# Reordering the prologue of an attention-and-MLP kernel: query transpositions ahead of the last value sums, with more dummy matmuls between

## The chip, the cores and the metric

The kernel runs on one core of one Trainium2 chip. The metric is the device time of one execution in microseconds (us), as the median of several runs. A profile of one execution shows, for each engine, when every instruction ran: TensorE (PE, and PEld for its weight loads), VectorE (DVE), ScalarE (ACT), GpSimd (POOL) and SyncE (SP).

## The reference

Eight batches of eight heads, 576 queries each, head size 64. Keys and values are averaged over groups of eight rows first, so that 72 pooled rows remain. Attention over them gives the input of an MLP with a SiLU:

```python
def _attn_ref(q, k, v):
    pool = 8
    k_p = k.reshape(B, H, Sp, pool, D).mean(axis=3)
    v_p = v.reshape(B, H, Sp, pool, D).mean(axis=3)
    scores = scale * np.matmul(q, k_p.transpose(0, 1, 3, 2))
    attn = softmax(scores)            # over the 72 pooled keys
    return np.matmul(attn, v_p)       # (8, 8, 576, 64)

x = attn_out.transpose(0, 2, 1, 3).reshape(4608, 512)
h = x @ w_in                          # 512 -> 2048
out = (h * sigmoid(h)) @ w_out        # 2048 -> 512
```

## The kernel before

The MLP walks over 4608 tokens in nine tiles of 512 (loop `for t in range(NT)`); each tile has an up stage (`up`, w_in and SiLU) and a down stage (`down` in the first tile, `down_quarters` after it). A batch is 576 tokens, so the attention of the next batch is run inside the MLP of the current tile: its steps are `fillers` with due times, which `spread` puts between the MLP matmuls. Nothing else is scheduled: `tc.manual_schedule()` leaves the instructions of every engine in the order in which the code issues them, and semaphores alone hold an engine back.

The attention of batch 0 has no MLP to hide in. It is the prologue (lines 705 to 770), and its order is written out by hand. The 576 queries are treated as two halves `f` of 288 columns, the eight heads as two groups `g` (or `a`) of four. `part(g, f)` is one quarter of the work. For each quarter:

- `q_transpose(b, a, f)` (L153, DVE) puts queries into `qT`.
- `scores(b, segs)` (L351, PE) multiplies `qT` with pooled keys `kz` into four PSUM tiles `sc_ps`, one per head, and ACT takes four exponentials into `es` (L359).
- `denominators` (L369, PE) sums `es` over the pooled keys. Reciprocals are taken on ACT as exp(-ln) (L378, L379), or on DVE (L375) for the second query half.
- `numerators` (L395, PE) multiplies `es` with pooled values `vp`, and DVE multiplies by the reciprocals into `xT` (L404), the input of the MLP. The first MLP tile begins with columns 0 to 287, the first query half; the second half's denominators and numerators are fillers of its up stage.

Keys and values are pooled by DVE additions in `slot_sums(name, j)` (L274, L278): rows lie in five slots of 128, slots 0 to 2 are `j=0`, the others `j=1`. `select_k(b, a)` (L296) and `select_v(b, a)` (L314) are small matmuls that pick the rows of four heads into PSUM, and `copy_k` (L303) and `copy_v` (L321) bring them to `kz` and `vp`; each call says whether ACT (`act_copy`) or DVE copies.

`warm_up(n)` issues n dummy matmuls of 128x512 on zeros into a PSUM tile that nobody reads (L703). The prologue holds 37 of them.

PSUM has three buffers under the tag `mm` (dummies, hidden tiles `hp_ps`, some numerators) and five under `at` (scores, denominators, other numerators). A tile takes the next buffer of its tag in turn, and waits until that buffer's last reader is done. In the prologue the `at` tiles are, in order of issue, one `kz_ps`, four scores, four scores, two denominators, and so on, so the scores of one quarter follow the readers of earlier ones.

Transfers of the prologue are issued ahead of all this by SP, ACT and POOL (queries by POOL, in four pieces; values by POOL in three). On ACT the exponentials and the SiLU belong to different table sets; `moe_tables()` loads the second one (L414) ahead of the first up stage.

Of the kernel before, what the change touches and what calls it, by code (L numbers as in the profile page):

```python
# [36 lines left out]
def kernel(  # L37
# [53 lines left out]
    def ps_tile(shape, dtype, tag, name):  # L91
        return psum.tile(shape, dtype, tag=tag, bufs=banks[tag], name=name)
# [57 lines left out]
    def q_transpose(b, a, f):  # L150
        st = batches[b]
        n = QF * D
        nc.vector.transpose(  # L153
            out=st["qT"][:, a, f * QF : (f + 1) * QF].rearrange("r i c p -> r (i c p)"),
            in_=st["q_bf"][:, a, f * n : (f + 1) * n],
        )
# [94 lines left out]
    def load_slots(eng, b, name, i0, i1, half=None):  # L251
        es = slice(0, RE) if half is None else slice(half * RE // 2, (half + 1) * RE // 2)
        src = (k if name == "k" else v)[b].rearrange("h (sp p) d -> (h sp) (p d)", p=POOL)
        src = src[:, es]
        how = dict(accum_op=ALU.add) if half else {}
        tiles = row_tiles[name]
        w = es.stop - es.start
        if i0 == SLOTS:
            eng.dma_start(
                out=tiles[1][:REST, SLOTS - SA, :w], in_=src[128 * SLOTS :], **how  # L260
            )
        else:
            j = i0 // SA
            eng.dma_start(
                out=tiles[j][:, i0 - SA * j : i1 - SA * j, :w],
                in_=src[128 * i0 : 128 * i1].rearrange("(i r) e -> r i e", r=128), **how
            )

    def slot_sums(name, j, halves=False):
        raw = row_tiles[name][j]  # L270
        dst = rows5[name][:, SA:] if j else rows5[name][:, :SA]
        w = RE // 4 if halves else RE // 2
        while w > D:
            nc.vector.tensor_add(  # L274
                out=raw[..., :w], in0=raw[..., :w], in1=raw[..., w : 2 * w]
            )
            w //= 2
        nc.vector.tensor_add(out=dst, in0=raw[..., :D], in1=raw[..., D : 2 * D])  # L278


    def segments(h):
        r = SP * h
        while r < SP * (h + 1):
            i = r // 128
            e = min(SP * (h + 1), 128 * (i + 1))
            yield i, (128 if i < SLOTS else REST), r - 128 * i, r - SP * h, e - r
            r = e

    def select_k(b, a):
        st = batches[b]  # L290
        if a == 0:
            st["kz_ps"] = ps_tile([128, 2, 2, SP], FP32, "at", "kz_ps")
        for c in range(2):
            for s in range(4):
                for i, n, r, sp, m in segments(4 * a + s):
                    nc.tensor.matmul(  # L296
                        st["kz_ps"][32 * s : 32 * (s + 1), a, c, sp : sp + m],
                        lhsT=k5[:n, i, c * DH : (c + 1) * DH],
                        rhs=ident[:n, r : r + m], start=True, stop=True,
                    )  # L300

    def copy_k(b, a, copy=nc.vector.tensor_copy):
        copy(out=kz[b % 2][:, a], in_=batches[b]["kz_ps"][:, a])  # L303

    def select_v(b, a, tag="at"):
        st = batches[b]
        if a == 0:
            st["v_ps"] = ps_tile([128, H, D], FP32, tag, "v_ps")
            st["vp"] = mid.tile([SP, H, D], BF16, tag="vp", name="vp")
        for h in range(4 * a, 4 * (a + 1)):  # L310
            segs = list(segments(h))
            for j, (i, n, r, sp, m) in enumerate(segs):
                x = SP + r - sp
                nc.tensor.matmul(  # L314
                    st["v_ps"][:SP, h, :], lhsT=shifts[:n, x : x + SP], rhs=v5[:n, i],
                    start=(j == 0), stop=(j == len(segs) - 1),
                )

    def copy_v(b, a, copy=nc.vector.tensor_copy):
        hs = slice(4 * a, 4 * (a + 1))  # L320
        copy(out=batches[b]["vp"][:, hs, :], in_=batches[b]["v_ps"][:SP, hs, :])  # L321
# [3 lines left out]
    def part(g, f):  # L325
        return ((g, f * QF, (f + 1) * QF),)
# [6 lines left out]
    def width(segs):  # L333
        return QP * sum(i1 - i0 for _, i0, i1 in segs)

    def seg_cols(segs):
        o = 0
        for g, i0, i1 in segs:
            n = QP * (i1 - i0)
            yield g, i0, i1, slice(o, o + n)  # L340
            o += n

    def scores(b, segs):
        st = batches[b]
        w = width(segs)
        sc = [ps_tile([128, 512], FP32, "at", "sc_ps")[:SP, :w] for s in range(4)]
        for g, i0, i1, cs in seg_cols(segs):
            for c in range(2):
                for s in range(4):
                    rows = slice(32 * s, 32 * (s + 1))  # L350
                    nc.tensor.matmul(  # L351
                        sc[s][:, cs],
                        lhsT=kz[b % 2][rows, g, c, :],
                        rhs=st["qT"][rows, g, i0:i1, c, :],
                        start=(c == 0), stop=(c == 1),
                    )
        es = mid.tile([SP, 4, VW], BF16, tag="es", bufs=4, name="es")[:, :, :w]
        for s in range(4):
            nc.scalar.activation(es[:, s, :], sc[s], func=AF.Exp, scale=score_scale)  # L359
        st["es", segs] = es  # L360


    def denominators(b, segs, on_dve=False):
        st = batches[b]
        w = width(segs)
        es = st["es", segs]
        den_ps = ps_tile([128, 512], FP32, "at", "den_ps")
        for s in range(4):
            nc.tensor.matmul(  # L369
                den_ps[32 * s : 32 * (s + 1), :w],  # L370
                lhsT=ones, rhs=es[:, s, :], start=True, stop=True,
            )
        rec = mid.tile([128, VW], FP32, tag="rec", bufs=4, name="rec")[:, :w]
        if on_dve:
            nc.vector.reciprocal(rec, den_ps[:, :w])  # L375
        else:
            lnd = mid.tile([128, VW], FP32, tag="lnd", name="lnd")[:, :w]
            nc.scalar.activation(lnd, den_ps[:, :w], func=AF.Ln)  # L378
            nc.scalar.activation(rec, lnd, func=AF.Exp, scale=-1.0)  # L379
        st["rec", segs] = rec  # L380

    def numerators(b, segs, tags=("at", "at")):
        st = batches[b]
        w = width(segs)
        g0, i0, i1 = segs[0]
        c0 = b * S % NX + i0 * QP
        cols = slice(c0, c0 + (i1 - i0) * QP)
        es = st.pop(("es", segs))
        rec = st.pop(("rec", segs))
        nu = []  # L390
        for c in range(2):
            nu_ps = ps_tile([128, 512], FP32, tags[c], "nu_ps")
            for g, _, _, cs in seg_cols(segs):
                for s in range(4):
                    nc.tensor.matmul(  # L395
                        nu_ps[32 * s : 32 * (s + 1), cs],
                        lhsT=st["vp"][:, 4 * g + s, c::2],
                        rhs=es[:, s, cs],
                        start=True, stop=True,
                    )  # L400
            nu.append(nu_ps)
        ng = len(segs)
        for c in range(2):
            nc.vector.tensor_mul(  # L404
                out=xT[:, 2 * g0 + c : 2 * (g0 + ng - 1) + c + 1 : 2, cols],
                in0=nu[c][:, :w].rearrange("r (g n) -> r g n", g=ng),
                in1=rec.rearrange("r (g n) -> r g n", g=ng),
            )
# [292 lines left out]
    def warm_up(n):  # L701
        for _ in range(n):
            nc.tensor.matmul(warm_ps, lhsT=warm[:, :128], rhs=warm, start=True, stop=True)  # L703
# [33 lines left out]
    act_copy = nc.scalar.copy  # L737
# [3 lines left out]
    copy_k(0, 0, act_copy)  # L741
    warm_up(4)
    q_transpose(0, 0, 0)
    scores(0, part(0, 0))
    slot_sums("k", 1)
    warm_up(3)
    select_k(0, 1)
    copy_k(0, 1, act_copy)
    q_transpose(0, 1, 0)
    warm_up(2)  # L750
    scores(0, part(1, 0))
    denominators(0, part(0, 0))
    slot_sums("v", 0)
    warm_up(2)
    select_v(0, 0, "mm")
    copy_v(0, 0, act_copy)
    denominators(0, part(1, 0))
    q_transpose(0, 0, 1)
    scores(0, part(0, 1))
    slot_sums("v", 1)  # L760
    warm_up(1)
    numerators(0, part(0, 0), ("mm", "at"))
    warm_up(2)
    select_v(0, 1, "mm")
    copy_v(0, 1)
    q_transpose(0, 1, 1)
    warm_up(2)
    numerators(0, part(1, 0), ("mm", "at"))
    scores(0, part(1, 1))
    warm_up(2)  # L770
    load_slots(nc.gpsimd, 1, "k", 0, 3)
    load_slots(nc.gpsimd, 1, "k", 3, 4)
    load_slots(nc.gpsimd, 1, "k", 4, 5)
# [147 lines left out]
```

## Time and profile before

| | |
|---|---|
| median of 3 runs | 289.03 us (288.86 to 289.22) |
| profiled execution | 288.86 us, its span 287.0 us |
| PE busy | 279.4 us, 97% of the span |
| DVE busy | 225.6 us, 79% |
| ACT busy | 183.4 us, 64% |
| POOL busy | 52.6 us, 18% |
| first MLP matmul (L546) starts | 18.12 us after the span's start |
| fourth hidden tile of the up stage starts | 20.85 us |
| PE's granted clock | full in all 40 slices |

The span is the time from the first to the last instruction of the program on the core; the execution's own time also holds what lies around it. Busy time of PE is modelled from the starts of pipelined matmuls, so two neighbouring matmuls can overlap in it; starts are more reliable than ends. A chain of waits is the sequence of work that ended last, followed back from the last instruction, at each step to what released it. In the records a few matmuls can be missing: 35 dummy matmuls are recorded, with 37 weight loads for them.

### The profile page before, as it was taken

The numbers are of one execution on the slowest core, as the hardware profiler recorded it, in microseconds if no ns is written. First come the engines' busy times: TensorE is split into PE (matmuls) and PEld (weight loads), VectorE is DVE, ScalarE is ACT, GpSimd is POOL, SyncE is SP. The second block draws the span as 40 slices with busy tenths as digits, with TensorE's granted clock in tenths as the row PEclk, the third lists the DMA queues.
The fourth block names the chain that finished last, engine by engine and source line by source line (L and its number), as shares of the span: only waits on it lengthen the run. The fifth ranks groups of instructions, "written<-read, shape, count | busy, mean of one in ns | idle before, by whom it ended". The sixth has DMA issues, their size and how long they took to land.

```text
span 287.0 us, 6919 instructions
## 1 busy us (share of the span) xinstructions
PE 279.4 (97%) x2773; PEld 196.0 (68%) x2793; DVE 225.6 (79%) x403; ACT 183.4 (64%) x359; POOL 52.6 (18%) x68
## 2 busy tenths in 40 slices
PE   8989999999999999999999999999999999999995
PEld 2438544466777677767888886687667867786684
DVE  3987854979969896979797969886988786846773
ACT  1577676468656876688568857794679558325700
POOL 8754317501020011101020107212000000000000
PEclk9999999999999999999999999999999999999999
DMA  8999999893749566973979396968830032006004
GB/s 210 269 262 231 217 310 172 221 216 53 148 67 208 124 91 106 136 209 60 140 122 211 73 151 112 164 121 162 161 77 0 2 86 63 2 5 142 2 1 148
DMA packets 35296, 37.70 MB, mean 131 GB/s; under 512 B 9952, under 2 KB 27616, under 8 KB 35264
## 3 DMA queue, kind: packets, MB, share of 16 engines
q0 software_dynamic: 21760, 20.86, 43.1%
q1 hardware_dynamic: 12928, 15.48, 22.3%
q10 hardware_dynamic: 576, 0.92, 1.1%
q8 instruction: 22, 0.36, 0.6%
q14 instruction: 10, 0.08, 0.1%
HBM read 36.70 MB, written 9.44 MB: 161 GB/s over the span
## 4 chain that ended last, share of the span: by engine, by line
PE 91%; DVE 4%; ACT 2%; issue 1%; DVEq 0%
PE hp_ps L546 23%; PE o_psP L654 15%; PE o_psQ L654 15%; PE u_psQ L488 7%; PE u_psP L488 6%; PE o_psR L654 5%; PE sc_ps L351 4%; PE warm_ps L703 4%; PE o_ps L581 3%; PE nu_ps L395 3%; PE den_ps L369 2%; PE u_psR L488 2%; DVE rr_sb L508 1%; ACT r_sb L505 1%; DVE w_sum L632 1%
## 5 line engine op out<-in xcount | busy, mean ns | idle before, releaser
L546 PE MATMUL hp_ps<-xT,w_in_sb 128*128 128x512 bf16 (+3 forms) x397 | 80.8, 338 | 1.4 <-ACT h_T L552 0.4
L552 ACT ACTIVATE h_T<-hp_ps 128x512 bf16<-128x512 f32 (+2 forms) x95 | 51.3, 545 | 27.2 <-PE hp_ps L546 26.3
L654 PEld LDWEIGHTS <-h_sum 128*128 128x128 bf16 x640 | 60.6, 98 | 11.9 <-issue 1.3
L546 PEld LDWEIGHTS <-w_in_sb 128*128 128x128 bf16 x412 | 39.3, 98 | 24.9 <-issue 1.4
L614 DVE TENSOR_TENSOR h_sum<-h_T 128x1024 bf16<-128x1024 bf16 (+1 forms) x72 | 50.8, 743 | 7.0 <-ACT h_T L552 7.0
L359 ACT ACTIVATE es<-sc_ps 72x384 bf16<-72x384 f32 (+1 forms) x100 | 39.0, 470 | 10.0 <-PE sc_ps L351 10.0
L488 PEld LDWEIGHTS <-w_sum 128*128 128x128 bf16 x300 | 29.3, 98 | 8.2 <-DVE x_sum L455 0.5
L654 PEld LDWEIGHTS <-h_T 128*128 128x128 bf16 x256 | 24.1, 98 | 4.4 <-issue 0.9
L496 ACT ACTIVATE h_T<-c_sb 128x512 bf16<-128x512 f32 x30 | 18.8, 628 | 11.6 <-DVE c_sb L520 11.6
L404 DVE TENSOR_TENSOR xT<-nu_ps,rec 128x384 bf16<-128x384 f32 (+1 forms) x50 | 24.0, 533 | 0.4
L378 ACT ACTIVATE lnd<-den_ps 128x384 f32<-128x384 f32 (+1 forms) x23 | 11.1, 484 | 20.2 <-PE den_ps L369 20.2
L153 DVE STREAM_TRANSPOSE qT<-q_bf 128x576 bf16<-128x576 bf16 x32 | 23.0, 754 | 0.0
L182 POOL DMA_DIRECT2D raw<-in_k_dram x5 | 7.0, 1405 | 66.3 <-DVE qT L153 31.2
L274 DVE TENSOR_TENSOR raw<-raw 128x384 f32<-128x384 f32 (+3 forms) x20 | 12.3, 616 | 7.2 <-DMA raw<-in_v_dram 3.6
L654 PE MATMUL o_psP<-w_out_sb,h_sum 128*128 128x256 bf16 x128 | 17.6, 273 | 0.0
L654 PE MATMUL o_psQ<-w_sum,h_sum 128*128 128x256 bf16 x128 | 16.7, 273 | 0.0
L654 PE MATMUL o_psQ<-w_out_sb,h_sum 128*128 128x256 bf16 x128 | 16.6, 273 | 0.0
L654 PE MATMUL o_psP<-w_sum,h_T 128*128 128x256 bf16 x128 | 16.5, 273 | 0.0
L654 PE MATMUL o_psQ<-w_sum,h_T 128*128 128x256 bf16 x128 | 16.5, 273 | 0.0
L182 POOL DMA_DIRECT2D raw<-in_v_dram x5 | 6.9, 1390 | 49.4 <-DMA raw<-in_v_dram 15.6
L654 PE MATMUL o_psR<-w_sum,h_sum 128*128 128x256 bf16 x128 | 15.7, 273 | 0.0
L558 POOL DMA_DIRECT2D out_dram<-o_sb x1 | 0.6, 628 | 81.8 <-issue 81.8
(77 smaller groups left out, 435.9 us busy)
## 6 DMA issues: line engine op xcount, KB each, us to landing
out_dram<-o_sb SPq DMA_DIRECT2D x128, 64.0 KB, 3.0
q_bf<-in_q_dram POOLq DMA_DIRECT2D x6, 576.0 KB, 11.1
raw<-in_k_dram SPq DMA_DIRECT2D x6, 512.0 KB, 5.7
raw<-in_k_dram POOLq DMA_DIRECT2D x5, 576.0 KB, 9.6
raw<-in_v_dram POOLq DMA_DIRECT2D x5, 576.0 KB, 9.1
raw<-in_v_dram SPq DMA_DIRECT2D x5, 512.0 KB, 8.2
w_in_sb<-in_moe_w_in_dram POOLq DMA_DIRECT2D x8, 256.0 KB, 8.3
w_out_sb<-in_moe_w_out_dram POOLq DMA_DIRECT2D x4, 512.0 KB, 13.8
```

The source lines that it names most:

```text
L153: nc.vector.transpose(out=st["qT"][:, a, f * QF : (f + 1) * QF].rearrange("r i c p -> r (i c p)"), in_=st["q_bf"][:, a, f * n : (f + 1) * n],)
L182: nc.gpsimd.dma_start(out=batches[b][f"{name}_raw"], in_=source(b, name)[:, :, PH:], accum_op=ALU.add,)
L274: nc.vector.tensor_add(out=raw[..., :w], in0=raw[..., :w], in1=raw[..., w : 2 * w])
L351: nc.tensor.matmul(sc[s][:, cs], lhsT=kz[b % 2][rows, g, c, :], rhs=st["qT"][rows, g, i0:i1, c, :], start=(c == 0), stop=(c == 1),)
L359: nc.scalar.activation(es[:, s, :], sc[s], func=AF.Exp, scale=score_scale)
L404: nc.vector.tensor_mul(out=xT[:, 2 * g0 + c : 2 * (g0 + ng - 1) + c + 1 : 2, cols], in0=nu[c][:, :w].rearrange("r (g n) -> r g n", g=ng), ...
L488: nc.tensor.matmul(ps[bank][:, u, :], lhsT=w[:, kk, 128 * u : 128 * (u + 1)], rhs=x[:, kk, :], start=first and u == 0 and kk == 0, stop=kk ...
L496: nc.scalar.activation(h_T[:, g : g + 2, j * NQ : (j + 1) * NQ], src, func=AF.Silu)
L546: nc.tensor.matmul(hp_ps[:, r0:r1], lhsT=w_in_sb[:, kk, g * 128 : (g + 1) * 128], rhs=xT[:, kk, x0 : x0 + r1 - r0], start=(kk == 0), stop= ...
L552: nc.scalar.activation(h_T[:, g, n0 : n0 + n], hp_ps[:, :n], func=AF.Silu)
L614: nc.vector.tensor_tensor(out=h_sum[n][:, ks, :], in0=quarter(*a, ks), in1=quarter(*b, ks), op=op)
L654: nc.tensor.matmul(ps[b][:, c, :], lhsT=left(n, kt, c), rhs=W_OUT[n][:, kt, :], start=b not in begun, stop=kt == k1 - 1, skip_group_check= ...
```

## The change

Four things in the prologue change; the rest of the kernel is the same text, and its instructions stand in the same order.

- `scores` takes a callable `between`, which it calls ahead of its fourth exponential. The first scores use it for the sums, selection and ACT copy of the second half of the keys. PE's and DVE's orders stay as they were there; on ACT that copy moves ahead of the fourth exponential.
- The first value copy goes from ACT to DVE and stands behind the transposition `q_transpose(0, 1, 1)`, ahead of `slot_sums("v", 1)`.
- On DVE both transpositions of the second query half stand ahead of that copy and of `slot_sums("v", 1)`. Before, the second of them stood behind these sums, two products and the second value copy.
- On PE the last scores, `part(1, 1)`, move ahead of `select_v(0, 1)` and the numerators of `part(1, 0)`; before, they were behind both. Dummy matmuls are spread otherwise: 45 in place of 37.

```diff
-    def scores(b, segs):
+    def scores(b, segs, between=None):
...
         for s in range(4):
+            if s == 3 and between:
+                between()
             nc.scalar.activation(es[:, s, :], sc[s], func=AF.Exp, scale=score_scale)
...
     q_transpose(0, 0, 0)
-    scores(0, part(0, 0))
-    slot_sums("k", 1)
-    warm_up(3)
-    select_k(0, 1)
-    copy_k(0, 1, act_copy)
+
+    def rest_k():
+        slot_sums("k", 1)
+        warm_up(3)
+        select_k(0, 1)
+        copy_k(0, 1, act_copy)
+
+    scores(0, part(0, 0), rest_k)
     q_transpose(0, 1, 0)
     warm_up(2)
     scores(0, part(1, 0))
     denominators(0, part(0, 0))
     slot_sums("v", 0)
-    warm_up(2)
+    warm_up(3)
     select_v(0, 0, "mm")
-    copy_v(0, 0, act_copy)
+    q_transpose(0, 0, 1)
     denominators(0, part(1, 0))
-    q_transpose(0, 0, 1)
+    warm_up(1)
     scores(0, part(0, 1))
+    warm_up(3)
+    q_transpose(0, 1, 1)
+    copy_v(0, 0)
     slot_sums("v", 1)
+    numerators(0, part(0, 0), ("mm", "at"))
     warm_up(1)
-    numerators(0, part(0, 0), ("mm", "at"))
-    warm_up(2)
+    scores(0, part(1, 1))
+    warm_up(4)
     select_v(0, 1, "mm")
     copy_v(0, 1)
-    q_transpose(0, 1, 1)
     warm_up(2)
     numerators(0, part(1, 0), ("mm", "at"))
-    scores(0, part(1, 1))
-    warm_up(2)
+    warm_up(3)
```

## The prediction, made before the result was known

> **What bounds the kernel now.** The page first: engine shares, then the slices.
>
> ```profile
> PE 279.4 (97%) x2773; PEld 196.0 (68%) x2793; DVE 225.6 (79%) x403; ACT 183.4 (64%) x359; POOL 52.6 (18%) x68
> ...
> PE   8989999999999999999999999999999999999995
> ...
> PEclk9999999999999999999999999999999999999999
> ```
>
> TensorE is busy 97% of the span, at full granted clock in every slice; the only thin slices are the first few and the last. The change sits in the prologue, up to about 20 us, so the question is whether the stream that follows can absorb a shift. The table by stages (columns: window, its length, busy us of PE, PEld, DVE, ACT, POOL, clock, DMA share, GB/s) answers that, together with the list of what PE waited for from 21 us to the end, of which the second longest entry is shown after it (engine, line, releaser: us in total, times, longest):
>
> ```profile
> 12.10:18.10 6.00, 5.51 (x64) 2.42 (x62) 4.95 (x11) 4.56 (x15) 3.97 (x6) 1.00 1.22 200
> 18.10:20.85 2.75, 2.35 (x22) 1.22 (x20) 2.03 (x2) 2.72 (x7) 1.48 (x2) 1.00 1.17 296
> 20.85:35.20 14.35, 14.30 (x135) 9.81 (x136) 11.43 (x23) 10.13 (x25) 5.75 (x9) 1.00 1.19 229
> ```
>
> ```profile
> PE u_psR L488 <- ACT r_sb L505: 0.2, 1, 0.2
> ```
>
> From 20.85 us PE is full (14.30 of 14.35), and after that its waits are a few tenths, on engines that themselves follow PE; none is a wait for a transfer. So the time at which PE gets past the last prologue wait, 20.85 us, moves the end one for one. I then read the chain of waits through that stretch (start, length, what):
>
> ```profile
> 13.54 0.28 PE den_ps L369
> 13.82 0.41 PE sc_ps L351 x8
> 14.24 0.32 PE warm_ps L703
> ...
> 14.57 0.61 PE nu_ps L395 x8
> 15.19 0.54 PE warm_ps L703 x2
> 15.72 0.33 PE v_ps L314 x6
> ...
> 16.15 0.42 DVE vp L321
> 16.57 0.70 DVE qT L153
> ...
> 17.31 0.48 PE sc_ps L351 x8
> 17.79 1.29 ACT es L359 x4
> ...
> 19.09 1.28 ACT L414
> ...
> 20.39 0.42 ACT h_T L552
> ...
> 20.85 0.41 PE hp_ps L546 x2
> ```
>
> The chain leaves PE at 16.15: the copy of the second value half, the last query transposition, the last scores, their four exponentials, the table load, the first SiLU. Then PE, out of PSUM for a fourth hidden tile, goes on at 20.85.
>
> **Paces.** Start to start in the timeline of PE: a dummy 0.22 us (two from 17.68 to 18.12); eight scores 0.37 (17.31 to 17.68), 0.08 more when dummies stand ahead (four dummies 8.53 to 9.49, 0.96); eight numerators 0.36; six value selections 0.33 (chain). From the first MLP matmul (18.12) to the point where the fourth hidden tile could begin PE needs 2.16 (the third tile's last matmul starts at 20.16, its successor could 0.12 later; the stretch includes both fillers of denominators). On ACT: an exponential 0.29 apart and 0.41 long; ln, then its exponential 0.45 later, the next instruction 0.35 after that. On DVE: transposition 0.77 long, 0.70 apart.
>
> **What PE waits for now, from 13.54 (last denominator matmul) to 20.85, 7.31 us.** Work: rest of that matmul 0.21, scores 0.37, seven dummies 1.54, two numerator groups 0.72, value selection 0.33, scores 0.37, MLP 2.16: 5.70. So 1.61 is waiting: 0.18 for the first value copy on ACT (14.39 to 14.57), 0.19 for a PSUM bank held by a logarithm, 0.21 for the second value copy, 0.33 for the transposition, 0.57 for the SiLU, 0.13 in uneven issue.
>
> **The change, part by part.**
> *Third exponential and K copy.* The copy of the second K half is put ahead of the fourth exponential of the first scores. It now starts 11.29, when its matmuls (ending 11.26) release it, and that exponential ended 11.26: the copy cannot start sooner. The exponential moves to about 11.5 to 11.9; the denominators that read it start 12.10, so it costs nothing; without that 0.2 us of cover it would delay them one for one. Gain nothing.
> *Value copy from ACT to DVE.* ACT loses 0.25 (14.17 to 14.42), so the second ln starts 14.17, and the next exponentials 14.96 instead of 15.21, the last ending 16.26. DVE does two transpositions from 12.23 (the query half is needed by 12.93, and DVE's transfer wait of 0.46 at 13.0 is filled by it), then the copy to about 14.1, then the last value sums, 1.48 long, to 15.6 instead of 14.93. Queued behind them are the first products, needed by nobody before the first MLP matmul. All DVE extras are covered: PE wants the copy at 15.08 and the sums at 17.5.
> *Dummies.* 37 become 45. One of the eight falls into the wait for exponentials that ends at 13.54; seven, 1.54 us, come after it.
> *PE's new order.* From PE free at 13.75: dummy and scores(0,1) to 14.42, three dummies to 15.08, numerators to 15.44, a dummy, scores(1,1) at 15.74. These need the PSUM banks of the exponentials above: the fourth bank is free at 16.26, PE issues at 16.30, and goes on at 16.65 (second half, 0.14 plus 0.21) where 16.11 was possible: a new wait of 0.54. It is bounded below by 0 (ACT ahead), above by 0.79 (without the 0.25 that ACT saves); I take 0.54, since every ACT term is a row. Then four dummies to 17.53 and the value selection to 17.86. As now, 0.10 passes before the copy and 0.05 after its 0.42, so numerators start at 18.47, where two dummies end at 18.30: wait 0.17 (between 0 and 0.21, today's). Numerators to 18.83, three dummies, first MLP matmul at 19.49, 1.37 later than now. The products that it reads end 1.34 after the numerators begin, 19.81; the third MLP matmul, the first to read the second head group, comes behind a denominator group at 20.07. No wait.
> *ACT's end.* Last exponentials 16.76 to 18.06, table load to 19.36: 1.0 earlier than now. The first hidden tile is summed only at 20.74, so SiLU waits for PE, and the fourth hidden tile starts unhindered at 19.49 + 2.16 = 21.65.
> *Sum.* 21.65 - 20.85 = +0.80. By the ledger: seven dummies 1.54, two switches 0.16, waits 0.71 instead of 1.61: again +0.80. What is late next: reciprocals on DVE start 1.3 later; the K sums of the next batch then end at about 28.6, the selections that read them come at 28.57 and 29.65 plus 0.80, the first needing only the first sums (27.3). Covered by 0.8 to 2 us. POOL's transfers keep their order and wait for transfers up to 33 us.
>
> **Two rules weighed.** The granted clock reads 1.00 in all stages, and dummies have the same 0.22 us after a 0.33 us wait as before it. The Trainium skill, "TensorE: Matmul & The Clock Gate", Part 1 (HAM oscillation), says that the clock falls only after PE idles for a window of about 3.4 us; it speaks against this change, as the longest wait here is 0.57, so by it a dummy buys nothing; were clock at stake, each such window at half speed would cost 1.7. The table load shows as 1.28, starting 0.02 after the exponentials. "ScalarE: Activation LUTs" (What ACT_TABLE_LOAD costs) adds a drain, 2.66 in all; by that the load would end at 20.72, still ahead of 20.74, and the sum would not move.
>
> **Rivals.**
> *Dummies are free (faster).* If the seven after 13.54 run beside the groups that follow, PE is 1.54 earlier, the MLP begins at about 17.95, and the fourth hidden tile at 20.11: -0.74. For: PE's waits show 1.61 us that could hold them. Against: they stand in order, seven of them behind the new waits, at 0.22 each. It turns faster as soon as the first MLP matmul starts before 18.69. 288.3 us.
> *The new PSUM wait is absent (no change).* 0.80 - 0.54 = +0.26, 289.3. For: it hangs on one ScalarE sequence. Against: its banks' order is fixed by the program.
> *Both ends lose (much slower).* The 0.57 wait is not saved but comes back as a wait for late vector results (reciprocals, K sums): +1.37, 290.4. For: DVE has no gap from 20 to 28.6. Against: the covers above.
> That the change doesn't do what it says isn't open: the built order shows both transpositions ahead of the sums and 45 dummies.
>
> **How the numbers follow.** The profiled execution took 288.86 us around its span of 287.0, 0.17 below the median of 289.03; 288.86 + 0.80 = 289.66 for it, 289.83 as median. 0.2%, about what a measurement of this kernel can tell from no change, is 0.58. Forecast 0.70, its own range 289.4 to 290.3 (waits at their bounds, uneven issue of 0.1 to 0.2 per group); free dummies 0.08; absent wait 0.12; both ends lose 0.10. The forecast's lower end falls within 0.58 for about 0.10 of its 0.70. Faster 0.08, same 0.22, slower 0.70. Range 289.0 to 290.6.
>
> **What would show it.** After: scores(1,1) held by ACT near 16.3; table load over near 19.4; first MLP matmul near 19.5; no SiLU wait at its fourth tile; that tile near 21.65; 45 dummy weight loads; clock 1.00. Wrong if the first MLP matmul comes before 18.7, or PE shows new waits after 22 us.

## The result, and the profile after

| | before | changed |
|---|---|---|
| median (6 runs each) | 288.91 us (287.84 to 289.22) | 290.44 us (289.72 to 290.75) |
| ratio | | 1.0057 (1.0035 to 1.0079) |
| profiled execution, its span | 288.86 us, 287.0 us | 290.32 us, 288.2 us |

The changed kernel is slower, by about 1.5 us where 0.80 was forecast. The median lies in the range given, 289.0 to 290.6, but above the narrower 289.4 to 290.3 that the prediction gave its own sum. What the sum forecast and the rest of the difference can be read apart.

First the profile of the changed kernel: page, then the stages (same columns as before, cut at its own marks), then what PE waited for from 21 us on.

```profile
PE 280.0 (97%) x2781; PEld 196.2 (68%) x2801; DVE 225.9 (78%) x404; ACT 183.4 (64%) x358; POOL 52.4 (18%) x68
...
PE   7999999999999999999999999999899999999995
...
PEclk9999999999999999999999999999999999999999
```

```profile
18.66:20.82 2.16, 2.16 (x22) 1.22 (x21) 1.70 (x2) 0.71 (x2) 1.47 (x2) 1.00 1.15 347
20.82:35.20 14.38, 14.33 (x138) 9.81 (x137) 12.02 (x25) 10.11 (x25) 5.61 (x9) 1.00 1.19 226
```

```profile
PE u_psR L490 <- DVE x_sum L457: 1.1, 2, 0.7
```

The first MLP tiles now run without any gap (2.16 busy of 2.16), but a wait for the input sums `x_sum`, 1.1 us in two places, is new, and the twenty-ninth slice shows it: an 8, at 202 to 209 us.

Then the prologue, PE's timeline of the changed kernel (start, length, engine, line, what, count, idle before):

```profile
7.42 0.28 PE L296 MATMUL kz_ps<-shifts,k 128*32 128x72 bf16 x12 [0.50 <-DVE k L278]
...
15.05 0.80 PE L351 MATMUL sc_ps<-qT,kz 32*72 32x288 bf16 x8
16.00 0.81 PE L705 MATMUL warm_ps<-warm 128*128 128x512 bf16 x3 [0.16 <-issue]
16.65 0.48 PE L314 MATMUL v_ps<-v,shifts 128*72 128x64 bf16 x6
17.06 0.61 PE L705 MATMUL warm_ps<-warm 128*128 128x512 bf16 x2
17.64 0.43 PE L397 MATMUL nu_ps<-es,vp 72*32 72x288 bf16 x8
18.00 0.82 PE L705 MATMUL warm_ps<-warm 128*128 128x512 bf16 x3
18.66 0.41 PE L548 MATMUL hp_ps<-xT,w_in_sb 128*128 128x288 bf16 x2
```

and ACT's, same columns:

```profile
14.11 1.28 ACT L361 ACTIVATE es<-sc_ps 72x288 bf16<-72x288 f32 x4
15.79 1.30 ACT L361 ACTIVATE es<-sc_ps 72x288 bf16<-72x288 f32 x4 [0.40 <-PE sc_ps L351]
17.11 1.28 ACT L416 ACT_TABLE_LOAD   x1
19.69 0.41 ACT L554 ACTIVATE h_T<-hp_ps 128x288 bf16<-128x288 f32 x1 [1.30 <-PE hp_ps L548]
```

The absolute times can't be set beside those of before: here the first key selection starts at 7.42 us, there at 8.32, because the 19 dummies ahead of it reach their full pace sooner. Counted from it, the fourth hidden tile starts 12.53 us later before (20.85) and 13.40 later now (20.82). So the prologue costs 0.87 more, and in this profile the earlier head hid it: at 20.8 us the two kernels are level. The 1.27 us by which the profiled spans differ arise after that, most of them at the two waits for input sums.

### The profile page after: what moved, and what is told of

Read it like the earlier page. It is cut to its first block, busy times and chain, and to the rows that moved or that the text cites. A ratio compares the mean times of both kernels' runs of the same rounds, so it can differ in the third digit from the quotient of the medians.

```text
span 288.2 us, 6934 instructions
## 1 busy us (share of the span) xinstructions
PE 280.0 (97%) x2781; PEld 196.2 (68%) x2801; DVE 225.9 (78%) x404; ACT 183.4 (64%) x358; POOL 52.4 (18%) x68
## 5 line engine op out<-in xcount | busy, mean ns | idle before, releaser
L548 PEld LDWEIGHTS <-w_in_sb 128*128 128x128 bf16 x412 | 39.3, 98 | 24.4 <-issue 0.8
L182 POOL DMA_DIRECT2D raw<-in_k_dram x5 | 7.0, 1404 | 68.6 <-DMA raw<-in_k_dram 29.7
L490 PEld LDWEIGHTS <-w_in_sb 128*128 128x128 bf16 x120 | 11.7, 97 | 6.0 <-issue 2.0
L182 POOL DMA_DIRECT2D raw<-in_v_dram x5 | 6.9, 1389 | 47.5 <-DVE raw L188 23.3
```

The source lines that it names most:

```text
L182: nc.gpsimd.dma_start(out=batches[b][f"{name}_raw"], in_=source(b, name)[:, :, PH:], accum_op=ALU.add,)
L490: nc.tensor.matmul(ps[bank][:, u, :], lhsT=w[:, kk, 128 * u : 128 * (u + 1)], rhs=x[:, kk, :], start=first and u == 0 and kk == 0, stop=kk ...
L548: nc.tensor.matmul(hp_ps[:, r0:r1], lhsT=w_in_sb[:, kk, g * 128 : (g + 1) * 128], rhs=xT[:, kk, x0 : x0 + r1 - r0], start=(kk == 0), stop= ...
```

## The experiments

Times are medians; a ratio is to the kernel before, on the same chip, with its 95% interval. The experiments' runs were made in three groups on three chips, on which the kernel before took 288.67, 289.03 and 289.33 us, so two times from different groups are compared more safely by their ratios. Two lengths are taken from each trace: *prologue*, from the first key selection to the start of the fourth hidden tile, and *rest*, from there to the start of the last matmul. Theory P: the prologue costs the forecast's 0.8 and the rest of the difference is late waits for keys. Theory C: the change itself lengthens the later work. Theory S: the prologue costs all of it.

**Both kernels again.** No edit.

> The changed kernel once more. Theory P (the prologue costs +0.8 us, the rest of the measured +1.5 is lost later, where VectorE waits for the keys of a later batch ahead of the sums that TensorE wants): about 290.4 us; from the first key selection matmul to the fourth hidden tile about 13.4 us, as in the first profile, against 12.5 in the kernel before; waits of TensorE for the input sums of 0 to 1 us in some tiles, not necessarily in the same ones. Theory C (the late waits come from the change): the same waits of 0.4 and 0.7 us near 146 and 206 us again.

> The kernel before once more, for a second profile of it. Theory P: about 288.9 us, prologue stretch 12.5 us, and waits for the input sums of up to 1 us in some tile can appear here too. Theory C: none over 0.3 us. A ratio of 1.000 to the kernel before shows what the timing can tell apart.

> The changed kernel a third time, beside the kernel before on the same chip. Theory P: between the kernel before plus 0.8 us and the 1.5 us measured twice, since late waits for keys come on top and fall by chance; the stretch from the fourth hidden tile to the last matmul between 261.9 (no late wait) and 264.5 us, prologue 13.3 to 13.4. Theory C (the change makes the late waits longer): again 1.4 us or more over the kernel before.

| | time | ratio | prologue | rest |
|---|---|---|---|---|
| before, first profile | 288.91 | | 12.53 | 262.55 |
| before again | 288.85 | 1.0005 (0.9987 to 1.0023) | 12.53 | 264.30 |
| changed, first profile | 290.44 | 1.0057 (1.0035 to 1.0079) | 13.40 | 263.85 |
| changed again | 290.41 | 1.0054 (1.0033 to 1.0075) | 13.33 | 262.99 |
| changed, third time | 290.31 | 1.0033 (1.0009 to 1.0058) | 13.33 | 263.22 |

The prologue is steady to 0.07 us, the rest varies by 1.75 us, and its longest value is that of the kernel *before*. PE's longest wait in that trace, and VectorE's for keys (in total, times, longest):

```profile
PE u_psR L488 <- DVE x_sum L455: 1.5, 2, 1.2
```

```profile
DVE raw L188 <- DMA raw<-in_k_dram: 2.1, 2, 1.5
```

and what stands around 204 us there, on VectorE's timeline:

```profile
203.89 1.22 DVE L188 TENSOR_TENSOR raw<-raw 72x1024 f32<-72x1024 f32 x1 [1.48 <-DMA raw<-in_k_dram]
205.14 0.76 DVE L193 TENSOR_TENSOR kp<-raw 72x256 bf16<-72x256 f32 x2
205.82 0.68 DVE L689 TENSOR_TENSOR o_sb<-o_psQ,t_sb 128x512 f32<-128x512 f32 x1
206.42 1.75 DVE L455 TENSOR_TENSOR x_sum<-xT 128x512 bf16<-128x512 bf16 x5
```

In these rows VectorE takes its instructions in the order of the code. The additions that pool the next keys (L188) wait 1.48 us for a transfer, and the input sums, which TensorE needs and which need nothing of these keys, stand behind them. The wait near 146 us of the changed kernel's first profile (0.41 us) is there again in smaller size in its other two (0.15 and 0.28), but that of 206 us is not there in the second; the kernel before has its own near 117 (0.33) and 206 us (1.16). So C's "same waits" fell, though not its "1.4 us or more" in two of three comparisons.

**Key additions behind the input sums.** In both kernels:

```diff
-                for stage in range(2):
-                    f_down.append((100, lambda stage=stage: pool_k(a + 1, stage)))
-                f_up.append((0, lambda: load_one(a + 1, "k")))
-                f_up.append((1, lambda: load_q(a + 1)))
-                f_up.append((2, lambda: load_rest(a + 1, "k")))
+                f_up.append((8, lambda: load_one(a + 1, "k")))
+                f_up.append((9, lambda: load_q(a + 1)))
+                f_up.append((10, lambda: load_rest(a + 1, "k")))
+                for stage in range(2):
+                    f_up.append((8, lambda stage=stage: pool_k(a, stage)))
```

> The kernel before with the pooling additions of the next keys moved on VectorE from the end of a down stage to behind the five input sums of the next tile (the load of the keys after it moves behind them as well, by eight matmuls). Theory P: TensorE no longer waits over 0.15 us for the input sums; 0.2 to 0.8 us faster than the kernel before, 288.1 to 288.7. If the late waits cost nothing on the median: 288.9.

> The changed kernel with the same move of the key additions. Theory P: no waits for the input sums, and 0.8 us more than the kernel before with that move, so 289.0 to 289.5. Rival S (the prologue itself costs all of the measured +1.5): 1.5 us more than the kernel before with that move, 289.8 to 290.2.

Measured: 291.84 us, ratio 1.0103 (1.0078 to 1.0129), for the kernel before with it; 292.81 us, 1.0142 (1.0117 to 1.0168), for the changed one. The edit as such was a miss. It took away every wait for input sums, as intended, but put a fixed one in its place, the same in both kernels, shown from PE's waits in the changed one:

```profile
PE u_psQ L490 <- DVE rr_sb L510: 3.2, 5, 0.6
```

The additions now stand ahead of `rr_sb`, which reads a PSUM bank that TensorE's next product writes. As a comparison it is useful all the same, since the chance part is gone: rest 266.14 us in *both* traces, prologue 12.53 and 13.32, times 0.97 apart. S asked for 1.5. The times alone, six runs and five, leave room for that; the prologue lengths, 0.80 apart, do not.

**The keys on another queue.** The plain half of the keys is issued by SP, behind the output stores of the tile. In the first profile of before:

```profile
112.59 12.93 SPq L566 DMA_DIRECT2D out_dram<-o_sb  x16
125.91 1.17 SPq L173 DMA_DIRECT2D raw<-in_k_dram  x2
```

Sixteen stores occupy SP for 12.93 us, though the buffer of the keys is free 10 us earlier: the row of the edited kernel below issues the same load at 115.83. POOL stood idle then. The other half of the keys is a transfer that adds onto the plain half (`load_rest`, L182, on POOL's queue), so it has to follow it, and a late plain half makes all the keys late.

```diff
     def load_one(b, name):
-        load_rows(nc.sync, raw, source(b, name)[:, :, :PH])
+        load_rows(nc.gpsimd if name == "k" else nc.sync, raw, source(b, name)[:, :, :PH])
```

> The kernel before with the plain half of each later batch's keys issued on the POOL queue instead of behind the output stores on SP's; nothing else moves. Theory P (the late waits come from keys that land near the moment at which VectorE needs them): the keys land some 9 us earlier, TensorE's waits for the input sums fall to 0.15 us or less, the stretch from the fourth hidden tile to the last matmul is 262.2 to 262.6 us, and the time falls by 0.2 to 0.8 us, to 287.9 to 288.5. If the late waits have another source: 288.7 and the waits stay.

> The changed kernel with the same keys on the POOL queue. Theory P: 0.8 us more than the kernel before with that edit (288.7 to 289.3), and the same 262.2 to 262.6 us after the fourth hidden tile. Theory C (the change itself makes later work slower, by some 0.6 us): 1.4 us more than the kernel before with that edit, and a stretch after the fourth hidden tile that is 0.6 longer.

Measured: 287.87 us (287.53 to 288.22 in 12 runs), ratio 0.9960 (0.9942 to 0.9979), for the kernel before with it; 288.70 us (288.27 to 289.31), 0.9994 (0.9977 to 1.0011), for the changed one. The difference is 0.83 us. Rest: 261.91 and 261.90 us. Prologue 12.75 and 13.33 (in the first of these its value sums, which wait for their transfer, held it a little, the head being early). Both halves are issued earlier, on POOL's timeline in the first profile of before and then in the changed kernel with the edit:

```profile
132.16 1.40 POOL L182 DMA_DIRECT2D raw<-in_k_dram  x1 [16.23 <-DVE qT L153]
```

```profile
115.83 1.34 POOL L173 DMA_DIRECT2D raw<-in_k_dram  x2 [3.66 <-DVE kp L193]
124.64 1.43 POOL L182 DMA_DIRECT2D raw<-in_k_dram  x1 [6.71 <-issue]
```

Of PE's waits after 21 us only two issue gaps are left, in both kernels; the changed one's list is

```profile
PE hp_ps L548 <- issue: 0.2, 1, 0.2
PE o_ps L583 <- issue: 0.2, 1, 0.2
```

and VectorE's additions follow the products without a gap, on the changed kernel's timeline:

```profile
141.96 1.02 DVE L406 TENSOR_TENSOR xT<-nu_ps,rec 128x384 bf16<-128x384 f32 x2
142.90 1.21 DVE L188 TENSOR_TENSOR raw<-raw 72x1024 f32<-72x1024 f32 x1
```

This settles theory P for the mechanism: with the keys early, the change costs the forecast's 0.8 and passes to the end one for one. The highest of the twelve runs of the one, 288.22, lies below the lowest of the other, 288.27. It also shows that late keys cost the kernel before 1.2 us at the median (289.03 in the same runs, against 287.87), where its first profile showed 0.65 over the 261.9 that is left without them. That gain was larger than expected.

**Without seven dummies.** In the changed kernel the four ahead of the last value selection and the three ahead of the MLP are left out, with the keys on POOL, and with the keys as they were:

```diff
     scores(0, part(1, 1))
-    warm_up(4)
     select_v(0, 1, "mm")
...
     numerators(0, part(1, 0), ("mm", "at"))
-    warm_up(3)
```

> The changed kernel with keys on the POOL queue, and without the four dummies ahead of the last value selection and the three ahead of the MLP. By the dummies' rows (seven, 0.2 each): first key selection to fourth hidden tile 11.9 to 12.1 us instead of 13.35, 1.3 to 1.4 us less than with them, so 0.5 us less than the kernel before with that edit. Rival D (dummies cost nothing, or they hold the clock): no gain, or a granted clock under 1.

> The changed kernel without those seven dummies, keys left on SP's queue. By the dummies' rows 1.3 to 1.4 us less than the changed kernel, 288.9 to 289.1, with late waits as they fall; prologue stretch 11.9 to 12.1 us. Rival D: 290.4.

Measured: 287.46 us, ratio 0.9942 (0.9922 to 0.9962), with the keys on POOL, prologue 12.05, rest 261.90; 288.64 us, 0.9993 (0.9974 to 1.0012), with the keys on SP, prologue 12.06, rest 262.71. On POOL's queue the seven dummies are worth 1.24 us (288.70 - 287.46), and the prologue is 1.28 shorter; the dummies' rows gave 1.3 to 1.4. The granted clock of that run is 1.000. On SP's queue the difference to the changed kernel (another group's 290.44) is 1.8 us, more than the dummies explain; late waits fall on both sides of it, and nothing here shows how much of it they are. So the reordering by itself is a gain of about 0.4 us over the kernel before (287.46 against 287.87). The intervals of the two ratios overlap, but the prologue is 0.48 shorter than the usual 12.53. What makes the change slower is its dummies.

**Seven dummies in the old order.** The kernel before, keys on POOL:

```diff
-    warm_up(2)
+    warm_up(6)
     select_v(0, 1, "mm")
...
     scores(0, part(1, 1))
-    warm_up(2)
+    warm_up(5)
```

> The kernel before with keys on the POOL queue and seven more dummies: four ahead of the last value selection, three ahead of the MLP. By the path: the four lie on the chain value selection, value copy, transposition, last scores, exponentials, table load and cost their 0.87; the three fall into the 0.57 us that TensorE waits for the first SiLU and cost 0.1. Sum +0.7 to +0.95 over the kernel before with keys on the POOL queue: 288.6 to 288.8. If every dummy costs its length: +1.5, 289.4. If they are free: 287.9.

Measured: 288.61 us, ratio 0.9982 (0.9963 to 1.0001); 0.74 us over the kernel before with that queue, which was measured in another group (0.64 by the two ratios). Prologue 13.47, rest 261.92. The same number of dummies costs about half of their 1.5 us here (by the prologue 0.94 over the usual 12.53): those ahead of the MLP run into the wait for the first SiLU, and no gap is left ahead of the fourth hidden tile.

**The key copy put back.** The changed kernel, keys on POOL, with the first scores called as before, so that the copy of the second key half stands behind the fourth exponential.

> The changed kernel with keys on the POOL queue and the copy of the second key half put back behind the fourth exponential. The forecast costs this edit at nothing: 288.7, prologue 13.3 to 13.4 us. If the copy does start earlier in the changed kernel: up to 0.3 us slower without it.

Measured: 288.94 us, ratio 0.9995 (0.9975 to 1.0014), against 288.70 and 0.9994 with the move; prologue 13.33 in both. The two medians are of different groups, and 0.24 is within their intervals; the prologue shows nothing, as forecast.

**Fewer dummies at the head.** As without the seven, and `warm_up(19)` made `warm_up(15)`.

> The changed kernel with keys on the POOL queue, without the seven dummies ahead of the last value selection and the MLP, and with 15 instead of 19 dummies ahead of the first key selection. Where the first 19 end at 8.3 us the first key selection waits for TensorE, where they end at 7.0 for VectorE (7.4). With 15 it should start near 7.4 in every execution: 0 to 0.9 us saved, 287.0 to 287.3 as median against 287.5. If the 19 are needed for the clock: the dummies stay at 0.43 us apart longer, and the time rises over 287.5.

Measured: 287.33 us (287.00 to 288.79), ratio 0.9951 (0.9931 to 0.9972). The profiled execution shows the first key selection at 7.22, waiting for VectorE as intended, prologue 12.05, rest 261.92; but its ratio is no better than 0.9942 with 19, and its spread is wider. Inconclusive: the two ratios are of different groups, and their intervals overlap. Both beat the two kernels of this case.

## Why the prediction was right, and where it was short

*The waits that go and come.* Right. In the changed kernel PE comes to the last scores at 15.05 and leaves them at 15.78 (the next dummy's record is missing, its successor starts at 16.00, 0.22 later), where 0.37 is their length: a wait of 0.36 for the exponentials, 0.54 in the forecast. PE came there 0.21 later than worked out, counted from the first key selection; as only the later of PE and ACT counts, the shorter wait makes up for most of that. Shifted by the head's 0.90, the forecast's marks were 16.63 for the value selection, 17.57 for the numerators, 18.59 for the MLP, 20.75 for the fourth hidden tile; measured 16.65, 17.64, 18.66, 20.82.

*ACT's end.* Right: table load over at 18.39 (forecast 18.46 after the same shift), and SiLU waits 1.30 us for PE. No wait for SiLU is left on PE. The first hidden tile was summed 1.03 us after the MLP's start (18.66 to 19.69), not 1.25 as the forecast had it; that changed nothing. The Trainium skill ("ScalarE: Activation LUTs", What ACT_TABLE_LOAD costs) puts a drain of about 1.38 us beside the load. In the changed kernel nothing follows the load closely enough to tell; in the kernel before there is none on the path: the load of 1.28 began 0.02 us after the exponentials, and SiLU started 0.01 us after it.

*Dummies.* Right in size: seven cost 1.24 us by removal, against 1.54 less the waits that they would fill. The rival "dummies are free" falls with it, and with the old order, where they cost 0.74, since part of them filled a wait. Without them the longest wait of PE from 8 us on is 0.2 us and the granted clock 1.000. This agrees with the Trainium skill ("TensorE: Matmul & The Clock Gate", Part 1), by which the clock falls only after an idle window of about 3.4 us; the longest wait of PE in any run here is 1.2 us.

*The new PSUM wait is absent*: false, it is there. *Both ends lose*: false; no late reciprocals or key sums of the second batch show on PE. Its time, 290.4, is what was measured, by another cause.

*The signs of being wrong.* The prediction named two, and both appeared. The first MLP matmul came at 18.66, before 18.7; but this mark supposed that the head takes the same time in every execution, and the head was 0.90 earlier. Counted from the first key selection the MLP began after 11.24 us, where the forecast had 11.17 and free dummies 9.63. The other sign, new waits of PE after 22 us, is real, and the sum had no place for it.

*The step that failed* is the first one: "after that its waits are a few tenths, on engines that themselves follow PE; none is a wait for a transfer. So the time at which PE gets past the last prologue wait, 20.85 us, moves the end one for one." The profile of before did show VectorE waiting for keys at one place,

```profile
DVE raw L188 <- DMA raw<-in_k_dram: 0.6, 1, 0.6
```

and PE's 0.24 behind it was put down there to ACT. That was taken for a constant. It is the visible end of a transfer that lands close to its need in four tiles, and costs an execution anything from 0.65 to 2.4 us (the rest of five traces, less 261.9). In that profile the keys landed 2.6, 1.1 and 0.6 us ahead of their additions at 113, 143 and 172 us and held VectorE for 0.56 us at 202; in the second profile of the same kernel the keys of 113 us held it as well, for 0.65 us. With the loads on POOL's queue the keys of these four tiles landed 9 to 11 us ahead, in both kernels. The sum had no term for it, and the range only room for 0.8 of it. That the median still fell into the range is luck: 0.83 of the 1.5 us is what was forecast.

*What stays open.* 0.83 us is shown for the change. In the three comparisons with keys on SP's queue it was 1.0033 to 1.0057, which is 0.95 to 1.65 us; over all runs the medians are 290.37 (30 runs) and 289.03 (111 runs), 1.34 apart (means 1.23 apart; with keys on POOL's queue 0.92). Whether the changed kernel draws longer late waits on average, by 0.3 to 0.5 us, or met them by chance, these runs don't tell: in the traces the rest of the changed kernel (262.99 to 263.85) lies within that of the kernel before (262.55 to 264.30). No experiment here shows a way from the prologue to these transfers.

## What to carry to other kernels

Before a shift is passed on to the end one for one, look at every transfer that lands close to its first reader, in all tiles, and at what stands behind that reader on its engine: one profile shows one draw of it, and here one that landed 2.6 us ahead in one execution held its reader for 0.65 us in another. When a small change is to be measured, first take such a wait away in both kernels; here that cut the spread of twelve runs to 0.7 us in the kernel before and made the forecast's 0.8 visible at once. Dummy matmuls on an engine that is already the bound cost their length, unless a wait is there to hold them (here 1.24 us of 1.51, and 0.74 where a wait held more of them); a reordering that removes waits should remove the dummies that filled them, not add more.

## What the runs showed of the hardware that was not expected

The pace of the first dummies is 0.43 us and halves at a moment that differs between executions, so that 19 of them last 7.19 us in the first profile of the kernel before and 5.72 in that of the changed one:

```profile
1.20 7.19 PE L703 MATMUL warm_ps<-warm 128*128 128x512 bf16 x19 [1.20 <-DVE warm L716]
```

```profile
1.20 5.72 PE L705 MATMUL warm_ps<-warm 128*128 128x512 bf16 x19 [1.20 <-DVE warm L718]
```

The head of the kernel moves by 0.9 us with it, while the profile's clock row reads full in the first slice in both. The Trainium skill ("TensorE: Matmul & The Clock Gate", Part 1) says that the window which sets the clock runs freely, which would make it so; the rows show only the spread.

The order of transfers on one queue mattered more than the whole change to the prologue, and about as much as its seven dummies: the same two loads of keys, issued on an idle queue instead of behind sixteen stores, were worth 1.16 us in the kernel before, a ratio of 0.9960 (0.9942 to 0.9979).
